# A fused chunk attention and top-1 mixture of experts: the gathered rows are turned by a DRAM scratch and VectorE instead of TensorE

## The chip, the cores and the metric

The kernel runs on one core of a Trainium2 chip. The metric is the device time of one execution in microseconds; lower is better. The profile comes from one execution that the hardware profiler recorded.

## The reference

Attention works on 4 batches, 8 heads, 768 positions of 64 numbers. Chunks of 32 queries see 8 memory keys and up to 56 keys around the chunk. Its output is laid out as 3072 tokens of 512 numbers and goes into a mixture of 8 experts, of which each token takes one:

```python
logits = x @ w_gate + modality_bias[modality_id]
e_idx = np.argmax(logits, axis=1)
...
for e in range(E):
    mask = e_idx == e
    if not mask.any():
        continue
    h = np.maximum(x[mask] @ w1[e], 0.0)          # 512 -> 1024
    out[mask] = gate_w[mask, None] * (h @ w2[e])  # 1024 -> 512
```

All of it is float32. The outputs follow the inputs' draw: how many tokens an expert gets is known only on the chip.

## The kernel before

**Stages.** The first third of the time is attention and routing: TensorE, VectorE (DVE), ScalarE (ACT) and GpSimd (POOL) go through 32 half-units of heads, and the normalized outputs go to a DRAM tensor `xd`, one row of 512 numbers and a gate for each token. Behind that come the experts, in *rows of a plan*: one row is up to 256 tokens of one expert, and a *slot* is the stretch of the program in which TensorE computes one row while the other engines prepare the next. Row 0 and row 1 are prepared while attention and routing end and in the opening slot. `slot(2)` computes row 1 and prepares row 2, `slot(3)` computes row 2, and so on: rows 2, 3, `ROW_R1`, `ROW_X`, up to seven more (`nextra`, in nested `If` blocks), and two more at the end. Two small groups of 32 tokens (`rest`) ride along in two of the slots. Short slots (`short_slot`) are skipped for this input.

**A slot.** TensorE first runs `mm1(f)` for f = 0 to 7: 12 matmuls each, 128x128 weights against 256 tokens. Float32 accuracy comes from splitting each number into a high and a low float32r part (`wh`/`wl` for weights, `xth`/`xtl` for tokens, `hh`/`hl` for the hidden layer) and adding three products. Then `mm2(f)` for f = 0 to 7: 6 matmuls each against 512 columns. ACT and DVE split the weights (`conv`): those of `w2` during `mm1`, those of the next row's `w1` during `mm2` (`prepare`).

**Tokens.** POOL gathers the next row's 2 x 128 tokens from `xd` into `xg` (`gather`). They stand with a token on each partition, and `mm1` wants a feature on each. `trans`, called from `prepare` behind `mm2(2)` and `mm2(3)`, has TensorE turn 4 blocks of 128x128 into PSUM, from where ACT and DVE write `xth` and `xtl`. `trans_rest` does the same for 32 tokens.

**Order.** TensorE, SyncE (SP) and POOL follow the order of the code, and from the opening slot on ACT and DVE too. Weights come on SP's queue, eight DMAs of 256 KB for `w1` (`load_w(row, 0)`) and eight for `w2`. Each waits until its `raw` buffer has been converted. Each is conditional: where the plan has the same expert as the row before, the register `c` is 0 and no bytes move. In `begin`, POOL stores the finished row (`store`), waits for that store, copies indices and gates (`keep`) and gathers.

Of the kernel before, what the change touches and what calls it, by code (L numbers as in the profile page):

```python
# [53 lines left out]
def tile_chunk_attention_top1_moe(  # L54
# [676 lines left out]

    def trans(half):
# [5 lines left out]
        sl = slice(2 * half, 2 * half + 2)  # L738
        nc.scalar.copy(xth[:, sl, 0:256], t)  # L739
        nc.vector.tensor_sub(xtl[:, sl, 0:256], t, xth[:, sl, 0:256].bitcast(F32))  # L740

    def trans_rest(i):
        t = bank()[:, 0:4 * NR].rearrange("p (c n) -> p c n", c=4)
        for c in range(4):
            nc.tensor.transpose(t[:, c], xgr[i][:, c * P:(c + 1) * P], ident[0:NR, 0:NR])
        nc.scalar.copy(xth[:, :, 256:], t)
        nc.vector.tensor_sub(xtl[:, :, 256:], t, xth[:, :, 256:].bitcast(F32))
# [353 lines left out]
```

## Time and profile before

| | us |
|---|---|
| median of 3 runs | 457.82 |
| lowest and highest | 456.39, 460.05 |
| the profiled execution, its own time | 456.86 |
| its span, first to last instruction | 455.1 |

The span is what the profile's rows count from; 1.8 us of the execution lie around it. The profile names TensorE's matmuls PE, its weight loads PEld. PEclk is the granted TensorE clock as a share of 2.4 GHz.

### The profile page before, as it was taken

The numbers are of one execution on the slowest core, as the hardware profiler recorded it, in microseconds if no ns is written. First come the engines' busy times: TensorE is split into PE (matmuls) and PEld (weight loads), VectorE is DVE, ScalarE is ACT, GpSimd is POOL, SyncE is SP. The second block draws the span as 40 slices with busy tenths as digits, with TensorE's granted clock in tenths as the row PEclk, the third lists the DMA queues.
The fourth block names the chain that finished last, engine by engine and source line by source line (L and its number), as shares of the span: only waits on it lengthen the run. The fifth ranks groups of instructions, "written<-read, shape, count | busy, mean of one in ns | idle before, by whom it ended". The sixth has DMA issues, their size and how long they took to land. (4 is left out here: it accounts for less than half of the span.)

```text
span 455.1 us, 11712 instructions
## 1 busy us (share of the span) xinstructions
PE 426.9 (94%) x4009; PEld 360.7 (79%) x4009; DVE 309.9 (68%) x747; ACT 261.7 (58%) x524; POOL 194.6 (43%) x374
## 2 busy tenths in 40 slices
PE   7989997999975997999999999999999999999993
PEld 4667776777754886989796987989898988898982
DVE  7989796798884799848465455766667574848430
ACT  5758674685734663747366455656565665656421
POOL 8967679769784643314052221304040404040201
PEclk9999998999996899999999999999999999999998
DMA  7899999999859402177186824202662201111101
GB/s 198 155 218 239 210 238 191 242 192 195 183 137 247 171 1 88 54 209 238 39 234 231 237 73 161 94 0 95 172 210 83 89 5 53 44 50 46 46 2 46
DMA packets 74818, 61.66 MB, mean 135 GB/s; under 512 B 36091, under 2 KB 64979, under 8 KB 74740
## 3 DMA queue, kind: packets, MB, share of 16 engines
q1 hardware_dynamic: 68000, 41.50, 39.0%
q0 software_dynamic: 5888, 19.11, 14.0%
q8 instruction: 36, 0.59, 0.6%
q14 instruction: 42, 0.34, 0.3%
q10 hardware_dynamic: 852, 0.11, 0.2%
HBM read 77.43 MB, written 12.76 MB: 198 GB/s over the span
## 5 line engine op out<-in xcount | busy, mean ns | idle before, releaser
L756 PEld LDWEIGHTS tr<-xt,w 128*128 128x128 f32 x1152 | 143.0, 191 | 6.0 <-issue 2.2
L756 PE MATMUL tr<-xt,w 128*128 128x256 f32 (+1 forms) x1152 | 144.8, 287 | 2.9 <-PEq L1062 0.8
L766 PE MATMUL av<-wh,h 128*128 128x512 f32 x384 | 128.4, 400 | 0.0
L791 POOL DMA_INDIRECT out_dram<-o,ix_now x24 | 24.3, 1014 | 159.0 <-ACT o L787 157.7
L760 DVE SCALAR_TENSOR_TENSOR h<-tr,h 128x256 fp32r<-128x256 f32 x96 | 40.5, 423 | 73.0 <-ACT h L757 54.4
L766 PEld LDWEIGHTS av<-wh,h 128*128 128x128 f32 x384 | 72.3, 188 | 17.3 <-issue 1.7
L766 PE MATMUL av<-wl,h 128*128 128x512 f32 x192 | 75.8, 395 | 0.0
L289 POOL COPY vw<-vw 24x384 f32<-24x384 f32 (+1 forms) x128 | 61.7, 521 | 20.9 <-DMA vw<-in_v_dram 19.8
L704 DVE TENSOR_TENSOR w<-raw,w 128x512 fp32r<-128x512 f32 x94 | 60.3, 683 | 14.0 <-ACT w L702 13.9
L704 DVE TENSOR_TENSOR wl<-raw,wh 128x512 fp32r<-128x512 f32 x91 | 63.4, 698 | 7.5 <-ACT wh L702 0.2
L757 ACT ACTIVATE h<-tr 128x256 fp32r<-128x256 f32 x96 | 36.8, 385 | 53.0 <-PE tr L756 32.9
L702 ACT CAST wh<-raw 128x512 fp32r<-128x512 f32 x96 | 58.8, 615 | 0.0
L702 ACT CAST w<-raw 128x512 fp32r<-128x512 f32 x96 | 54.2, 624 | 5.0 <-DMA raw<-in_moe_w_dram 3.8
L787 ACT ACTIVATE o<-av,gate_now 128x512 f32<-128x512 f32 x24 | 16.2, 690 | 47.0 <-PE av L766 37.8
L766 PEld LDWEIGHTS av<-wl,h 128*128 128x128 f32 x192 | 36.2, 189 | 7.0
L331 ACT COPY kbd<-tr 64x672 f32<-64x672 f32 x47 | 36.6, 779 | 7.0 <-PE tr L325 4.0
L339 PE MATMUL sc<-kbd,qT 128*32 128x128 f32 x768 | 27.7, 277 | 5.4 <-POOL kbd L313 4.1
L359 ACT ACTIVATE PT<-tr 128x384 f32<-128x384 f32 x32 | 15.7, 492 | 28.4 <-PE tr L357 27.9
L719 POOL DMA_INDIRECT xg<-xd,gx x24 | 26.3, 1097 | 10.0 <-POOL gx L717 6.3
L369 PE MATMUL av<-vw,PT 128*32 128x130 f32 x768 | 29.3, 283 | 1.2 <-ACT PT L359 0.6
L339 PEld LDWEIGHTS sc<-kbd,qT 128*32 128x32 f32 x768 | 19.3, 109 | 10.9 <-POOL kbd L313 6.3
L739 ACT CAST xt<-tr 128x512 fp32r<-128x512 f32 x24 | 13.9, 586 | 22.0 <-PE tr L737 12.5
(238 smaller groups left out, 525.3 us busy)
## 6 DMA issues: line engine op xcount, KB each, us to landing
raw<-in_moe_w_dram SPq DMA_DIRECT2D x192, 256.0 KB
k<-in_k_dram SPq DMA_DIRECT2D x16, 384.0 KB
q<-in_q_dram SPq DMA_DIRECT2D x16, 384.0 KB
xd<-xb POOLq DMA_DIRECT2D x16, 384.0 KB, 6.4
vw<-in_v_dram SPq DMA_DIRECT2D x32, 184.0 KB
vw<-in_mem_v_dram SPq DMA_DIRECT2D x32, 48.0 KB
vw<-in_v_dram SPq DMA_DIRECT2D x32, 6.0 KB
vw<-in_v_dram SPq DMA_DIRECT2D x32, 2.0 KB
```

Of the source, the lines that this page charges most:

```text
L289: nc.gpsimd.tensor_copy(vw[r0:r0 + 24, c + 1:c + 1 + w, h, 0:D], vw[r0 + 32:r0 + 56, c:c + w, h, 0:D])
L331: copy(dst.rearrange("p c (i j) -> p c i j", j=2)[:, :, :, j], win)
L339: nc.tensor.matmul(sc[32 * j:32 * j + 32, t * P:(t + 1) * P], qT[:, 32 * c:32 * c + 32], kbd[:, c].rearrange("p h m -> p (h m)"), start=Tr ...
L369: nc.tensor.matmul(avb[32 * j:32 * j + 32, t * W:(t + 1) * W], PT[:, t * P + 32 * j:t * P + 32 * j + 32], vw[:, c].rearrange("p h d -> p ( ...
L702: nc.scalar.copy(wh[i], raw[i])
L704: (eng or nc.vector).tensor_sub(wl[i][:, s], raw[i][:, s], wh[i][:, s].bitcast(F32))
L719: nc.gpsimd.indirect_dma_start(out=xg[t], out_offset=None, in_=xd[0:rows], in_offset=bass.IndirectOffsetOnAxis(ap=gx[:, t:t + 1], axis=0))
L756: nc.tensor.matmul(pw, wt[f][:, c * P:(c + 1) * P], x[:, c, 0:w], start=(n == 0), stop=(n == 11))
L757: nc.scalar.activation(hh[:, f], ph, AF.Relu)
L760: nc.vector.scalar_tensor_tensor(hl[:, f], ph, 0.0, hh[:, f].bitcast(F32), op0=ALU.max, op1=ALU.subtract)
L766: nc.tensor.matmul(pos[t], x, w[8 + f], start=(f == 0 and n == 0), stop=(f == 7 and n == 2))
L791: nc.gpsimd.indirect_dma_start(out=out, out_offset=bass.IndirectOffsetOnAxis(ap=ix_now[:, t:t + 1], axis=0), in_=outs[t], in_offset=None, ...
```

## The change

Rows 0 and 1 stay as they were. From row 2 on (`NWHOLE`), `send` writes the gathered tokens to a DRAM scratch `xs`, and `fetch` reads them back in four DMAs, one for each quarter of the 512 features: partition 32a + s gets quarter a of tokens s, 32 + s, 64 + s and so on. `turn` (VectorE's transpose of 32x32 blocks) makes features of the partitions, and `turned` splits the result into `xth` and `xtl`. The features then stand in another order on the partitions, so `w1` is loaded to match: four DMAs for each half of the columns, each into 32 partitions with runs of 2 KB (before: 128 partitions, runs of 512 bytes). `conv` works on blocks of that layout, and `mm1` picks its blocks accordingly. Row 2 is the first in the new layout, so its `w1` is loaded without the condition. `send` and `fetch` stand on SP's queue, behind the loads of `w1` and between the two halves of those of `w2`. POOL copies and gathers ahead of the store now, with a second pair of index and gate tiles (`ix_out`, `gate_out`) for what is stored.

```diff
@@ load_w
-        kw = {} if row == 0 else {"cond": ev[row, "c"]}
-        for f in range(8):
-            if half == 0:
+        kw = {} if row == 0 or row == NWHOLE and half == 0 else {"cond": ev[row, "c"]}
+        for f in which:
+            if half == 0 and row < NWHOLE:
...
+            elif half == 0:
+                src = w1[ds(e, 1), :, (f // 4) * DM:(f // 4 + 1) * DM]
+                c = f % 4
+                nc.sync.dma_start(
+                    raw1[32 * c:32 * c + 32, f - c:f - c + 4],
+                    src[:, c * P:(c + 1) * P].rearrange("o (c s) f -> s (o c) f", s=32), **kw)
...
+    def split(x, sl, cols):
+        nc.scalar.copy(xth[:, sl, cols], x)
+        nc.vector.tensor_sub(xtl[:, sl, cols], x, xth[:, sl, cols].bitcast(F32))
+
+    def send(rest=None):
+        if rest is not None:
+            nc.sync.dma_start(xsr[rest], xgr[rest][:, 0:DM])
+        for t in range(2):
+            nc.sync.dma_start(xs[t * P:(t + 1) * P], xg[t][:, 0:DM])
+
+    def fetch(rest=None):
+        for a in range(4):
+            sl = slice(32 * a, 32 * a + 32)
+            if rest is not None:
+                nc.sync.dma_start(xqr[sl], xsr[rest][:, a * P:(a + 1) * P])
+            nc.sync.dma_start(xq[sl], xs[:, a * P:(a + 1) * P].rearrange("(j s) d -> s j d", s=32))
+
+    def turn(half):
+        nc.vector.transpose(
+            xv.rearrange("p c (t j s) -> p t j c s", t=2, j=4)[:, half],
+            xq[:, 4 * half:4 * half + 4].rearrange("p j (c s) -> p j c s", c=4))
+
+    def turned(half):
+        sl = slice(2 * half, 2 * half + 2)
+        split(xv[:, sl], sl, slice(0, 256))
...
-    def mm1(f, rest=False):
+    def mm1(f, rest=False, first=False):
...
-            nc.tensor.matmul(pw, wt[f][:, c * P:(c + 1) * P], x[:, c, 0:w], start=(n == 0), stop=(n == 11))
+            i, j = (f, c) if first else (f - f % 4 + c, f % 4)
+            nc.tensor.matmul(pw, wt[i][:, j * P:(j + 1) * P], x[:, c, 0:w], start=(n == 0), stop=(n == 11))
@@ begin
-        if not opening:
-            for t in range(2):
-                finish(t)
-            store()
-        keep()
-        if row is not None:
-            gather(row)
+        keep(opening)
+        if row is not None:
+            gather(row)
+        if not opening:
+            for t in range(2):
+                finish(t, gate_out)
+            store(ix_out)
@@ prepare
+        if f in (2, 3):
+            turn(f - 2)
         for i in ((0, 1), (2, 3), (4,), (5,), (6, 7))[f] if f < 5 else ():
             conv(i)
-        if f in (2, 3):
-            trans(f - 2)
+        if f in (3, 4):
+            turned(f - 3)
@@ slot
-                mm1(f, rest is not None)
+                mm1(f, rest is not None, row == NWHOLE)
                 conv(8 + f)
+                if row is not None and f == 0:
+                    send(rest_next)
+                if row is not None and f == 3:
+                    if rest is None:
+                        load_w(row, 1, range(4))
+                    fetch(rest_next)
```

On SP, at the place where row 2 is loaded, this stood before: the last two loads of `w1` (line 695) and the first of `w2` (line 699); `ISA` rows set the condition and address of the load behind them.

```order
L695 ISA
L695 DMA raw_2712<-in_moe_w_dram 128x4x128
L695 ISA
L695 DMA raw_2713<-in_moe_w_dram 128x4x128
L699 ISA
L699 DMA raw_2931<-in_moe_w_dram 128x512
```

Now the same place reads as below; line 752 is `send`, line 759 `fetch`, line 704 the new load of `w1`, line 708 that of `w2`.

```order
L704 DMA raw<-in_moe_w_dram 32x4x512
L752 DMA xs<-xg_2703 128x512
L752 DMA xs<-xg_2704 128x512
L708 ISA
...
L708 ISA
L708 DMA raw_2938<-in_moe_w_dram 128x512
L759 DMA xq<-xs 32x8x128 x4
L708 ISA
L708 DMA raw_2941<-in_moe_w_dram 128x512
```

Two DMAs to DRAM have come in ahead of the loads of `w2`, and four back from it between their halves.

On DVE, in the preparing half of a slot, this stood before (line 704 is `conv`, line 740 the low part of the tokens):

```order
L704 TENSOR_TENSOR w_2703<-raw_2709,w_2702 128x512
L704 TENSOR_TENSOR w_2703<-raw_2710,w_2702 128x512
L740 TENSOR_TENSOR xt_2701<-tr,xt_2700 128x2x256
L704 TENSOR_TENSOR w_2703<-raw_2711,w_2702 128x512
L740 TENSOR_TENSOR xt_2701<-tr,xt_2700 128x2x256
```

and now (line 713 is `conv`, 762 `turn`, 746 the low part of the tokens):

```order
L713 TENSOR_TENSOR w_2708<-raw,w_2707 128x512 x4
L762 STREAM_TRANSPOSE xv<-xq 128x4x4x32
L713 TENSOR_TENSOR w_2708<-raw,w_2707 128x512
L762 STREAM_TRANSPOSE xv<-xq 128x4x4x32
L713 TENSOR_TENSOR w_2708<-raw,w_2707 128x512
L746 TENSOR_TENSOR xt_2706<-xv,xt_2705 128x2x256
L713 TENSOR_TENSOR w_2708<-raw,w_2707 128x512 x2
L746 TENSOR_TENSOR xt_2706<-xv,xt_2705 128x2x256
```

Two transposes have come into DVE's row, and the second token split stands at its end, behind the last `conv`.

## Rows read from the trace of the kernel before

**Rows 1.** The page, busy time of the engines

```profile
PE 426.9 (94%) x4009; PEld 360.7 (79%) x4009; DVE 309.9 (68%) x747; ACT 261.7 (58%) x524; POOL 194.6 (43%) x374
```

**Rows 2.** The chain that ended last, one slot: start us, us, what

```profile
401.54 11.36 PE tr L756 x96
412.89 4.20 PE av L766 x18
417.10 0.44 PE tr L737 x4
417.53 1.40 PE av L766 x6
...
419.37 5.61 PE av L766 x24
```

**Rows 3.** Timeline of PE, starts of two slots and a slot's 32 more tokens

```profile
201.98 11.37 PE L756 MATMUL tr<-xt,w 128*128 128x256 f32 x96
...
219.20 0.60 PE L737 MATMUL tr<-ident,xg 128*128 128x128 f32 x4
...
220.09 0.50 PE L766 MATMUL av<-wh,h 128*128 128x512 f32 x1
...
306.84 11.52 PE L756 MATMUL tr<-xt,w 128*128 128x256 f32 x96
```

**Rows 4.** Timeline of DVE, a slot that starts at 306.84

```profile
313.70 0.69 DVE L704 TENSOR_TENSOR wl<-raw,wh 128x512 fp32r<-128x512 f32 x1
...
319.99 3.09 DVE L704 TENSOR_TENSOR w<-raw,w 128x512 fp32r<-128x512 f32 x5
...
326.15 1.28 DVE L704 TENSOR_TENSOR w<-raw,w 128x512 fp32r<-128x512 f32 x2
```

**Rows 5.** Groups by line, engine and shape: count, busy us, mean ns

```profile
L704 DVE TENSOR_TENSOR w<-raw,w 128x512 fp32r<-128x512 f32 x94 | 60.3, 683 | 14.0 <-ACT w L702 13.9
...
L294 DVE COPY qr<-q 128x768 f32<-128x768 f32 x16 | 9.9, 617 | 1.8 <-DMA q<-in_q_dram 1.8
```

**Rows 6.** Timeline of DVE: the last instruction of the plan

```profile
181.53 0.16 DVE L521 CAST regs<-rows 64x4 int32<-64x4 f32 x1
```

**Rows 7.** Timeline of SP's queue, issues of the loads of w1

```profile
182.91 3.01 SPq L695 DMA_DIRECT2D raw<-in_moe_w_dram  x8
...
226.20 6.44 SPq L695 DMA_DIRECT2D raw<-in_moe_w_dram  x8
```

**Rows 8.** Windows of 4 us: length, busy time of engines, PEclk, DMA share, GB/s

```profile
184.00:188.00 4.00, 4.00 (x36) 4.00 (x35) 3.22 (x6) 2.51 (x6) 2.96 (x6) 1.00 0.09 18
188.00:192.00 4.00, 4.00 (x27) 3.63 (x26) 3.24 (x7) 2.93 (x8) 0.36 (x1) 1.00 0.36 115
...
244.00:248.00 4.00, 4.00 (x18) 2.43 (x17) 2.50 (x4) 2.81 (x6) 0.00 (x0) 1.00 0.92 302
```

**Rows 9.** Issues by line: us from issue to landing

```profile
xg<-xd,gx POOLq DMA_INDIRECT x24, 3.5
```

**Rows 10.** Windows of 2 us in the attention, where loads go to 32 partitions

```profile
16.00:18.00 2.00, 2.00 (x40) 1.90 (x35) 1.97 (x5) 1.29 (x3) 1.96 (x2) 1.00 0.96 102
```

**Rows 11.** Windows of 2 us, where the granted clock falls and rises

```profile
140.00:142.00 2.00, 0.88 (x5) 0.68 (x4) 0.00 (x0) 0.00 (x0) 0.51 (x2) 0.55 1.08 314
...
146.00:148.00 2.00, 2.00 (x11) 2.00 (x11) 2.00 (x6) 1.53 (x3) 0.00 (x0) 0.50 0.81 287
...
150.00:152.00 2.00, 2.00 (x21) 1.24 (x20) 0.81 (x2) 1.22 (x4) 0.86 (x1) 0.89 1.01 374
```

**Rows 12.** Windows of 1 us behind the last matmul

```profile
447.00:448.00 1.00, 0.53 (x3) 0.09 (x1) 0.00 (x0) 0.29 (x1) 0.73 (x1) 1.00 0.00 0
...
449.00:450.00 1.00, 0.00 (x0) 0.00 (x0) 0.00 (x0) 0.00 (x0) 0.64 (x1) 1.00 0.48 193
...
451.00:452.00 1.00, 0.00 (x0) 0.00 (x0) 0.00 (x0) 0.00 (x0) 0.00 (x0) 0.50 0.00 0
```

**Rows 13.** Timeline of DVE, preparing in the slot with 32 tokens more

```profile
244.33 2.50 DVE L704 TENSOR_TENSOR w<-raw,w 128x512 fp32r<-128x512 f32 x4 [2.80 <-ACT w L702]
```

More of the change, by code (lines that the diff above doesn't have):

```diff
@@ L34 @@
 HEAD = 3
+NWHOLE = 2
 LAST = 3
@@ L85, in tile_chunk_attention_top1_moe @@
     xd = dram.tile([N, XW], F32, name="xd")
+    xs = dram.tile([2 * P, DM], F32, name="xs")
+    xsr = [dram.tile([NR, DM], F32, name=f"xsr{i}") for i in range(2)]
     qf = q.rearrange("b h s d -> (b h s) d")
@@ L674, in tile_chunk_attention_top1_moe, with load_w @@
     raw, wh, wl = [None] * 16, [None] * 16, [None] * 16
-    xp = hp = w1h = w1l = xg = xth = xtl = ix = gx = hh = hl = None
-    ix_now = const.tile([P, 2], I32, name="ix_now")
-    gate_now = const.tile([P, 2], F32, name="gate_now")
+    xp = hp = raw1 = w1h = w1l = xg = xth = xtl = ix = gx = hh = hl = None
+    ix_now, ix_out = [const.tile([P, 2], I32, name=f"ix_{i}") for i in range(2)]
+    gate_now, gate_out = [const.tile([P, 2], F32, name=f"gate_{i}") for i in range(2)]
     ev = {}
-    def load_w(row, half):
+    def load_w(row, half, which=range(8)):
         if half == 0:
@@ L704, in conv, with keep @@
             (eng or nc.vector).tensor_sub(wl[i][:, s], raw[i][:, s], wh[i][:, s].bitcast(F32))
-    def keep():
+    def keep(opening):
+        if not opening:
+            nc.gpsimd.tensor_copy(ix_out, ix_now)
+            nc.gpsimd.tensor_copy(gate_out, gate_now)
         nc.gpsimd.tensor_copy(ix_now, ix)
@@ L737, in trans, with turn_rest @@
                 nc.tensor.transpose(t[:, cc, tt * P:(tt + 1) * P], xg[tt][:, c * P:(c + 1) * P], ident)
[L738 to L747, printed above, removed]
-    def mm1(f, rest=False):
+        split(t, slice(2 * half, 2 * half + 2), slice(0, 256))
+    def turn_rest():
+        nc.vector.transpose(xvr, xqr.rearrange("p (c s) -> p c s", c=4))
+        split(xvr, slice(0, 4), slice(256, 256 + NR))
+    def mm1(f, rest=False, first=False):
         w = 256 + (NR if rest else 0)
@@ L802, in tail_mm1 @@
         for c in range(4):
-            wsl = [w[:, 4 * half:4 * half + 4, c * P:(c + 1) * P] for w in (w1h, w1l)]
+            wsl = [w[:, 4 * half + c] for w in (w1h, w1l)]
             for x, w in ((xth, wsl[0]), (xtl, wsl[0]), (xth, wsl[1])):
@@ L894, in tile_chunk_attention_top1_moe @@
         if i == n:
-            mm1(0)
+            mm1(0, first=True)
         if i > n:
-            mm1(1)
+            mm1(1, first=True)
         if i >= 2 and not first:
@@ L955, in tile_chunk_attention_top1_moe @@
     conv(5)
-    mm1(2)
+    mm1(2, first=True)
     pump(99, True)
@@ L960, in tile_chunk_attention_top1_moe @@
     for f in range(3, 6):
-        mm1(f)
+        mm1(f, first=True)
     for f in range(8, 16):
@@ L964, in tile_chunk_attention_top1_moe @@
     pump(99, True)
-    mm1(6)
-    mm1(7)
+    mm1(6, first=True)
+    mm1(7, first=True)
     pos = [ps.tile([P, 512], F32, name="av", tag="av", bufs=2) for _ in range(2)]
@@ L994, in slot @@
             for f in range(8):
-                mm1(f, rest is not None)
+                mm1(f, rest is not None, row == NWHOLE)
                 conv(8 + f)
-        if rest is None and row is not None:
+                if row is not None and f == 0:
[4 more added lines that the diff above has]
+                    fetch(rest_next)
+        if opening:
             load_w(row, 1)
+        elif rest is None and row is not None:
+            load_w(row, 1, range(4, 8))
         for f in range(6):
@@ L1035, in short_slot @@
             conv(f)
+        send()
         hr = [tail_mm1(0)]
@@ L1038, in short_slot @@
             conv(f)
-        load_w(row, 1)
+        load_w(row, 1, range(4))
+        fetch()
+        load_w(row, 1, range(4, 8))
         hr.append(tail_mm1(1))
```

23 lines of the change are left out of this document (14 added, 9 removed).

## The prediction

> **What bounds the kernel now.** I began with the page's busy times: TensorE is busy for 94% of the span, the next engine, DVE, for 68% [rows 1]. The chain of waits, followed back from the end, shows a slot of the experts as an unbroken run of TensorE work: 96 matmuls of `mm1` in 11.36 us (0.118 each), then 48 of `mm2` in 4.20 + 1.40 + 5.61 = 11.21 us, and two groups of four transposes, 0.44 us each [rows 2]. That is 23.45 us, and nothing else is on the path; the timeline agrees with it, so the slot that starts at 306.84 ends at 330.29. So in this stage an instruction taken from TensorE is worth its full time, as long as the next row's weights and tokens are ready at the slot's end.
>
> **What it removes.** The transposes of 10 slots (rows 2, 3, `ROW_R1`, `ROW_X`, four more, and two at the end): 10 x 2 x 0.44 = 8.8 us. In two of them 32 more tokens are turned: from the second group of transposes to the next `mm2` it takes 220.09 - 219.20 = 0.89 us [rows 3] against 0.44, so 0.45 each and 0.9 together. All of it lies on the path: **-9.7 us**. `mm1` and `mm2` keep their counts and shapes.
>
> **What DVE and ACT get.** In a common slot DVE starts on `conv` at 319.99 and is done at 326.15 + 1.28 = 327.43 [rows 4], with short waits for ACT between. Back to back its pitch is 3.09 / 5 = 0.62 us. Ten such pieces and two transposes of T end at 319.99 + 6.2 + 0.07 + 2T. They have to be done by the slot's new end, 330.29 - 0.88, plus 8 x 0.118 = 0.95, because `xtl` is first read by the ninth matmul: 330.36. So T may be 2.05 us before any slot waits. No row shows a transpose on DVE. A plain copy costs 0.41 us for 512 columns (617 ns for 768), a difference of 512 columns 0.68 [rows 5]; if it had to pass twice it were 1.37. I take 0.68, the row with the same size, and nothing on the path. The Trainium skill ("VectorE: DVE Perf Modes", The three transpose paths) gives 311 ns for a 128x128 bf16 transpose on DVE and says that it turns only blocks of 32x32; scaled to 512 columns that is an estimate of 1.24 us, under the limit too, and no run here shows it.
>
> **What the queue gets.** A row now sends 0.52 MB to DRAM and reads it back. In a slot that loads no weights nothing is ahead of these. In one that does, the fourth load of `w2` waits for the conversion that ends at 313.70 + 0.69 = 314.39 [rows 4], and `fetch` follows. 0.26 + 0.52 MB at the weights' rate of 302 GB/s [rows 8] take 2.6 us, and what is fixed of a DMA is 3.5 us to landing [rows 9] less the 0.87 us of its 0.26 MB, or 2.6: landing at about 319.6, with DVE at `turn` at 319.99 + 4 x 0.62 = 322.5. In the slot behind the skipped short slots, SP's first load goes out at 226.20 [rows 7], with 2.1 MB of `w1`, 1.05 MB of gather and store, and 0.59 MB of `send` ahead of `fetch`: 3.74 / 0.302 = 12.4 us and 2.6 fixed give 241.2; eight issues of `fetch` at 0.38 [rows 7] and 3.0 for the last make it 247.2. DVE is done with the fourth `conv` at 246.83 [rows 13]. The first comes in time, the second 0.4 us late, inside DVE's own slack of 2 x (2.05 - 0.68) = 2.7 us: **0**. The gather goes ahead of the store on POOL, so that it no longer waits for the store's landing; POOL is free enough [rows 1], and the store is late for nobody but the end, which is as before: **0**.
>
> **Where it pays: row 2.** This row's `w1` is now loaded whatever the plan says. Before, no bytes moved for it: in the 8 us behind its issues the DMA engines carried 18 and 115 GB/s [rows 8], 0.53 MB in all, less than the slot's gather and store (1.05 MB) come to. SP can't issue earlier, as it waits for the plan's registers, written by DVE at 181.53 [rows 6]; the first load goes out at 182.91 [rows 7]. From there everything stands in one line: 2.10 MB of `w1` with gather and store (1.05 MB) beside it, then `send` (0.52 MB), whose end `fetch` waits for. At 302 GB/s that is 3.67 / 0.302 = 12.2 us, and with 2.6 fixed `send` ends at 197.7. Four issues of `fetch` at 3.01 / 8 = 0.38 us [rows 7] and 3.0 for the last one's 0.13 MB give 202.2. In before, this slot ends at 201.98 [rows 3], now at 201.1 without a wait. But DVE stands in front of `turn(0)`, and behind it four conversions, two differences and one more transpose, eight pieces in all: 8 x 0.62 = 5.0 us, 207.2, and TensorE's eight matmuls that don't need the last part begin 0.95 earlier: 206.2. A wait of 206.2 - 201.1 = 5.1 us.
>
> That took the rate of a 128-partition load. The new `w1` and `fetch` write 32 partitions, 2.62 MB of them here. The nearest rows are far apart: 302 GB/s for 128 partitions with 2 KB runs [rows 8], 102 GB/s with the engines 0.96 busy where the attention's loads go to 32 partitions in runs of 256 bytes [rows 10]. I take 280, close to the first, since the runs have the lengths of the weights' loads and the DMA engines work by the run. Then 2.62 / 0.280 - 2.62 / 0.302 = 0.7 us come on top: **+5.8 us**.
>
> TensorE idles for some 4.9 us of that in one piece. Behind the kernel's last matmul (447.5) the granted clock still reads 1.00 in the window at 449 and 0.50 in that at 451 [rows 12], so idle stretches of that length cost the clock: half of 2.4 GHz. In the attention's end it fell in the window at 140 and rose in that at 150, with TensorE fully busy at 0.50 in the window at 146 [rows 11]. Some 4.4 us of matmuls at half speed (146 to 150.4, by the 0.89 of the last window) lose half of it: **+2.2 us**, between 0 (idle too short) and 5 (half of the ten microseconds from fall to rise).
>
> **The sum.** 456.86 - 9.7 + 5.8 + 2.2 = **455.2 us**. The profiled execution stood 0.96 us below the median of 457.82, 0.2%, inside the runs' own spread, so I leave the sum as it is. A measurement of this kernel can tell about 1%, 4.6 us, from no change: below 453.2 is faster, above 462.4 slower.
>
> **Rivals.**
>
> *Row 2 comes in time for the clock* (0.30). The 2.6 us fixed are taken from GpSimd's gathers, and SP's loads may need less; in the steady run of several loads some of it overlaps. With 1.3 less in `send` and in `fetch` each the wait is 5.8 - 2.6 = 3.2 us, TensorE's idle piece 2.3, at which the row at 449 still reads a full clock [rows 12]: 456.86 - 9.7 + 3.2 = 450.4, and up to 452 with a wait that is just too short for a fall.
>
> *Quarter loads run at two thirds* (0.18). What writes 32 partitions gets 200 GB/s, the middle of rows 8 and 10. Then the loads cost 2.62 x (5.0 - 3.31) = 4.4 us more, the wait is 9.5, and with the clock the time is 456.86 - 9.7 + 9.5 + 2.2 = 458.9; 457 to 460. For it speaks that the only 32-partition rows are slow, against it their short runs. The Trainium skill ("SBUF — State Buffer", Door 1: The DMA port swizzle) states that 32 partitions reach 8 of SBUF's 16 ports and measures 189 GB/s there against 328 for 128 partitions. By that rule this rival is what happens; no row of this trace shows such a load with long runs.
>
> *Slower: `fetch` late in the loading slots as well* (0.12). One mechanism, the same quarter loads at the 102 to 130 GB/s of rows 10, at the place of row 2: at 130 the 2.62 MB cost 20.2 us instead of 8.7, the wait grows to 16.6, and the slot at 226.20, whose spare is 2.3 us, waits some 9 more: 456.86 - 9.7 + 16.6 + 2.2 + 9 = 475. It decides from a wait of 12.1 us in row 2 on (12.1 + 2.2 - 9.7 = 4.6), that is from 167 GB/s down.
>
> **How the numbers follow.** The forecast has 0.40 and covers 453 to 457.5, a little of it below 453.2 (0.05). Faster by over 1%: 0.30 + 0.05 = 0.35. Within 1%: 0.35 + 0.18 = 0.53. Slower: 0.12. The range reaches over the first rival and the second: 449.5 to 460, which leaves out the slower one and some of the fastest.
>
> **What would show it.** In the changed profile: no transposes of tokens on TensorE past the opening slot; slots of 22.6 us in the chain; one long idle of TensorE near 201, with DVE's transpose waiting for `fetch` in it, then windows with the clock at 0.50; DVE's transposes under 1 us; no other wait of TensorE for tokens. Wrong it would be if DVE's transpose took over 2 us, if TensorE waited for DVE in every slot, or if row 2's tokens came before 198.

## The result, and the profile after

Forecast: 455.2 us. The changed kernel takes 462.62 us in the median of 14 runs (459.96 to 466.05), beside 457.1 for the kernel before in the same comparison; the ratio is 1.0118, 95% interval 1.0092 to 1.0145. So it is slower by 1.2%, outside the range.

The profiled execution took 460.86 us with a span of 459.1. Page, busy times [rows 1]:

```profile
PE 421.5 (92%) x3921; PEld 354.1 (77%) x3921; DVE 322.0 (70%) x769; ACT 261.7 (57%) x524; POOL 198.6 (43%) x396
```

TensorE has 5.4 us less to do and the kernel is longer: there must be new waits. The timeline of TensorE shows where they are (start us, us, engine, line, operation, tiles, count; in brackets the idle time ahead of it and what ended it), slot 3, the slot behind the skipped short slots (R1 from here on), and two common slots [rows 3]:

```profile
206.34 0.80 PE L790 MATMUL tr<-xt,w 128*128 128x256 f32 x2 [5.41 <-ACT xt L745]
207.90 14.07 PE L790 MATMUL tr<-xt,w 128*128 128x256 f32 x94 [0.76 <-ACT xt L745]
221.81 0.39 PE L800 MATMUL av<-wh,h 128*128 128x512 f32 x1
...
235.22 0.79 PE L790 MATMUL tr<-xt,w 128*128 128x288 f32 x4 [2.06 <-ACTq L1114]
238.00 13.67 PE L790 MATMUL tr<-xt,w 128*128 128x288 f32 x92 [1.99 <-DVEq L1114]
251.51 0.39 PE L800 MATMUL av<-wh,h 128*128 128x512 f32 x1
...
315.72 11.37 PE L790 MATMUL tr<-xt,w 128*128 128x256 f32 x96
338.12 11.38 PE L790 MATMUL tr<-xt,w 128*128 128x256 f32 x96
```

A common slot is now 338.12 - 315.72 = 22.40 us and was 23.41 to 23.44. Two places wait: ahead of slot 3, for row 2's tokens, 5.41 + 0.76 us; and at line 1114, where the short slots are skipped (the join from here on). There TensorE waits 2.06 us for ACT's queue, runs four matmuls and waits 1.99 us more for VectorE's queue; before, it waited 0.85. Behind the first wait, `mm1` takes 14.07 us for 94 matmuls instead of 11.37 for 96.

Before, `mm2` of slot 3 and of R1 started at

```profile
213.18 0.39 PE L766 MATMUL av<-wh,h 128*128 128x512 f32 x1
...
239.63 0.40 PE L766 MATMUL av<-wh,h 128*128 128x512 f32 x1
```

VectorE in front of both places, same columns:

```profile
203.68 0.71 DVE L762 STREAM_TRANSPOSE xv<-xq 128x512 f32<-128x512 f32 x1 [9.82 <-DMA xq<-xs]
...
228.11 0.71 DVE L762 STREAM_TRANSPOSE xv<-xq 128x512 f32<-128x512 f32 x1 [2.01 <-DMA xq<-xs]
...
233.78 0.68 DVE L746 TENSOR_TENSOR xt<-xv,xt 128x512 fp32r<-128x512 f32 x1
```

It waits for `fetch` in row 2 and again in slot 3. SP's queue of slot 2 and slot 3 (issue only; the landing is later) [rows 7]:

```profile
182.13 4.03 SPq L704 DMA_DIRECT2D raw<-in_moe_w_dram  x8
190.86 3.58 SPq L752 DMA_DIRECT2D xs<-xg  x2
194.79 1.39 SPq L708 DMA_DIRECT2D raw<-in_moe_w_dram  x4
197.85 1.81 SPq L759 DMA_DIRECT2D xq<-xs  x4
...
216.72 0.33 SPq L750 DMA_DIRECT2D xsr<-xgr  x1
217.14 0.88 SPq L752 DMA_DIRECT2D xs<-xg  x2
...
221.24 0.50 SPq L758 DMA_DIRECT2D xqr<-xsr  x1
...
225.14 0.32 SPq L759 DMA_DIRECT2D xq<-xs  x1
```

In slot 3, `send` goes out 216.72 - 206.34 = 10.4 us into the slot, because its first DMA takes the rest's 32 tokens (`xgr`), and these are gathered late, as GpSimd shows:

```profile
210.04 1.01 POOL L825 DMA_INDIRECT out_dram<-o,ix  x1 [0.30 <-issue]
...
211.85 1.12 POOL L741 DMA_INDIRECT xgr<-xd,gxr  x1 [0.28 <-POOL gxr L740]
```

The rest's gather stands behind the store of the slot's outputs. The windows (length, busy times, granted clock, DMA share, GB/s) of row 2's loads and of the idle piece behind them [rows 8, 11]:

```profile
184.00:186.00 2.00, 2.00 (x19) 2.00 (x18) 1.53 (x4) 1.39 (x4) 1.49 (x2) 1.00 1.07 230
...
190.00:192.00 2.00, 2.00 (x10) 1.60 (x9) 1.70 (x5) 2.00 (x5) 0.00 (x0) 1.00 1.07 204
204.00:206.40 2.40, 0.06 (x1) 0.06 (x1) 2.23 (x5) 0.73 (x2) 0.00 (x0) 0.50 1.07 241
206.00:214.00 8.00, 6.90 (x31) 6.60 (x32) 4.21 (x9) 4.79 (x10) 3.57 (x5) 0.51 0.89 215
214.00:218.00 4.00, 4.00 (x36) 4.00 (x35) 2.91 (x5) 1.99 (x5) 0.00 (x0) 1.00 0.39 112
```

From 184 to 192, while row 2's `w1` comes, the DMA engines are full (1.04 to 1.09) and move 204 to 231 GB/s. The clock reads 0.50 in the window at 204 and 0.51 from 206 to 214. Behind the join it is down again:

```profile
238.00:240.00 2.00, 2.00 (x8) 2.00 (x9) 0.00 (x0) 0.00 (x0) 1.39 (x3) 0.50 0.51 101
```

**Where the time went, slot by slot.** Lengths are differences between the first `mm1` matmuls of one slot and the next; X is the slot behind R1. I use them for all kernels below, since the attention stage, which the change doesn't touch, ends differently from one profiled execution to another (slot 2 starts between 176.8 and 185.8 us), so that spans of single executions don't compare. The ratios come from the repeated runs. The profiled executions of `e5_wide_w1` and `e13_both_orders` were slow ones, of which I read the slots and rates alone. All slots of a row come from one execution, and slots and ratios agree only to some 0.6% of the time (`e9a_pool_order`: its ten slots are 4.4 us shorter than before, 1.0% of the time; its ratio says 0.35%).

| kernel | slot 2 | slot 3 | R1 | X | these four | wait of TensorE at the join | median us, before's in the same comparison | ratio, 95% interval |
|---|---|---|---|---|---|---|---|---|
| before | 24.68 | 24.79 | 28.62 | 28.04 | 106.13 | 0.85 | | |
| after | 29.53 | 28.88 | 30.71 | 27.19 | 116.31 | 2.06 + 1.99 | 462.62, 457.1 | 1.0118 [1.0092, 1.0145] |
| e1_rest_gather_first | 28.49 | 26.54 | 30.44 | 28.59 | 114.06 | 0.52 + 1.09 | 459.63, 457.78 | 1.0048 [1.0009, 1.0087] |
| e2_first_new_row_3 | 24.55 | 29.01 | 31.81 | 27.19 | 112.56 | 6.44 + 1.11 | 459.38, 457.78 | 1.0042 [1.0011, 1.0073] |
| e3_both | 24.76 | 25.72 | 31.79 | 27.71 | 109.98 | 3.15 + 1.87 | 457.35, 457.78 | 0.9992 [0.9967, 1.0016] |
| e4_spin | 28.73 | 29.43 | 30.45 | 28.06 | 116.67 | 5.22 + 0.56 | 464.81, 457.78 | 1.0144 [1.0106, 1.0182] |
| e5_wide_w1 | 24.70 | 23.06 | 30.70 | 27.19 | 105.65 | 0.49 + 1.62 | 451.71, 457.74 | 0.9888 [0.9833, 0.9944] |
| e6_row2_conditional | 23.80 | 30.86 | 30.72 | 28.13 | 113.51 | 8.28 + 1.03 | 459.98, 457.74 | 1.0038 [0.9993, 1.0083] |
| e7_before_row2_loaded | 24.58 | 24.44 | 28.62 | 28.03 | 105.67 | 0.49 | 458.88, 457.74 | 1.0035 [0.9999, 1.0070] |
| e8_token_first | 24.72 | 28.96 | 31.19 | 28.20 | 113.07 | 6.39 + 0.99 | 461.21, 457.74 | 1.0094 [1.0057, 1.0130] |
| e9a_pool_order | 23.27 | 25.71 | 31.28 | 27.19 | 107.45 | 2.66 + 1.34 | 457.0, 457.77 | 0.9965 [0.9930, 1.0000] |
| e9b_pool_order_wide | 24.81 | 24.69 | 31.54 | 27.19 | 108.23 | 2.11 + 1.34 | 455.97, 457.77 | 0.9956 [0.9925, 0.9987] |
| e9d_pool_order_row3 | 24.76 | 24.88 | 31.73 | 27.19 | 108.56 | 2.30 + 1.67 | 456.7, 457.77 | 0.9955 [0.9923, 0.9986] |
| e10_join_load | 24.30 | 25.52 | 28.62 | 28.00 | 106.44 | 1.39 | 460.06, 457.77 | 1.0037 [1.0003, 1.0070] |
| e11_rest_on_pe | 23.79 | 24.36 | 27.82 | 27.21 | 103.18 | 0.75 | 451.96, 458.16 | 0.9874 [0.9821, 0.9927] |
| e12_fetch_early | 23.80 | 25.48 | 32.05 | 27.18 | 108.51 | 2.27 + 2.14 | 454.38, 458.16 | 0.9877 [0.9826, 0.9927] |
| e13_both_orders | 23.77 | 23.92 | 27.84 | 27.21 | 102.74 | 0.80 | 453.04, 458.16 | 0.9833 [0.9775, 0.9892] |

The other six slots took 141.38 us before and 135.84 after (22.40 to 23.13 each), and stay within 0.3 us in sum of 135.84 in every kernel that has the new transposes. All ten together: 247.51 before, 252.15 after, +4.6 us, which is the measured loss of 5.5 within what the stage ahead of them scatters.

### The profile page after: what moved, and what is told of

It is laid out like the page before. It is cut to its first block, busy times and chain, and to the rows that moved or that the text cites. A ratio compares the mean times of both kernels' runs of the same rounds, so it can differ in the third digit from the quotient of the medians.

```text
span 459.1 us, 11672 instructions
## 1 busy us (share of the span) xinstructions
PE 421.5 (92%) x3921; PEld 354.1 (77%) x3921; DVE 322.0 (70%) x769; ACT 261.7 (57%) x524; POOL 198.6 (43%) x396
## 5 line engine op out<-in xcount | busy, mean ns | idle before, releaser
L790 PE MATMUL tr<-xt,w 128*128 128x256 f32 (+1 forms) x1152 | 147.4, 289 | 11.6 <-ACT xt L745 6.2
L790 PEld LDWEIGHTS tr<-xt,w 128*128 128x128 f32 x1152 | 144.6, 193 | 15.6 <-ACT xt L745 7.3
L800 PE MATMUL av<-wh,h 128*128 128x512 f32 x384 | 124.0, 396 | 0.0
L825 POOL DMA_INDIRECT out_dram<-o,ix x24 | 24.2, 1010 | 97.0 <-ACT o L821 93.6
L711 ACT CAST w<-raw 128x512 fp32r<-128x512 f32 x96 | 53.1, 619 | 5.1 <-DMA raw<-in_moe_w_dram 5.0
L342 PE MATMUL sc<-kbd,qT 128*32 128x128 f32 x768 | 29.5, 290 | 6.0 <-POOL kbd L316 6.0
L821 ACT ACTIVATE o<-av,gate 128x512 f32<-128x512 f32 x24 | 16.1, 688 | 28.7 <-PE av L800 23.4
L342 PEld LDWEIGHTS sc<-kbd,qT 128*32 128x32 f32 x768 | 20.5, 114 | 12.0 <-POOL kbd L316 7.0
L745 ACT CAST xt<-xv 128x512 fp32r<-128x512 f32 x20 | 12.4, 619 | 25.3 <-DVE xv L762 25.3
```

Source lines behind the costliest of these rows:

```text
L342: nc.tensor.matmul(sc[32 * j:32 * j + 32, t * P:(t + 1) * P], qT[:, 32 * c:32 * c + 32], kbd[:, c].rearrange("p h m -> p (h m)"), start=Tr ...
L711: nc.scalar.copy(wh[i], raw[i])
L790: nc.tensor.matmul(pw, wt[i][:, j * P:(j + 1) * P], x[:, c, 0:w], start=(n == 0), stop=(n == 11))
L800: nc.tensor.matmul(pos[t], x, w[8 + f], start=(f == 0 and n == 0), stop=(f == 7 and n == 2))
L825: nc.gpsimd.indirect_dma_start(out=out, out_offset=bass.IndirectOffsetOnAxis(ap=to[:, t:t + 1], axis=0), in_=outs[t], in_offset=None, boun ...
```

## The experiments

My theory after the result (A in the expectations): the change does what it is for in every slot without loads, and loses that in two places, row 2's forced load, and the join, where the rest's late gather holds up `send` and so VectorE. The rivals: loads into 32 partitions are slow everywhere (B); VectorE has too much to do with two transposes more (C); or row 2 alone is the cause, through the clock that falls in its wait. The theory that came out at the end has three places in one chain: row 2's load, the slow loads into 32 partitions, and the rest's trip through the scratch.

**Undoing one part.** `e1_rest_gather_first` puts the rest's gather ahead of the store:

```diff
             gather(row)
+        if rest_next is not None:
+            gather_rest(rest_next)
         if not opening:
```

> The gather of the 32 more tokens goes ahead of the store on POOL. Theory A (two places of loss: row 2's forced load with the round trip behind it, and the join behind slot 3, where the late rest gather holds up send and so DVE): the first send of slot 3 leaves about 5 us earlier, DVE no longer waits 2.0 us for fetch, and TensorE's two waits at the join (2.06 and 1.99 us) and the clock's fall there shrink; the wait before slot 3 stays at 5.4 + 0.8. Time 3 to 4.5 us below the changed kernel's, so about 458 to 459.5. Theory B (what writes 32 partitions is slow everywhere): fetch stays late behind the loads, under 1 us gained. Theory C (DVE simply has too much to do with two transposes more): no change at the join.

`e2_first_new_row_3` leaves row 2 as it was before, with TensorE's transposes and a conditional load, and uses the new way from row 3 on:

```diff
-NWHOLE = 2
+NWHOLE = 3
...
-        if f in (2, 3):
+        if f in (2, 3) and row >= NWHOLE:
             turn(f - 2)
...
+        if f in (2, 3) and row < NWHOLE:
+            trans(f - 2)
```

> Row 3 instead of row 2 is the first in the new layout, row 2 is prepared as in the kernel before; row 3 has a new expert, so its unconditional load moves no byte more. Theory A: the 5.4 + 0.8 us wait and the half clock behind it (2.9 us) vanish, 0.9 us of transposes come back: 453 to 456, a ratio to the kernel before of about 0.99 to 1.0. Theory B: row 3's w1 and fetch are quarter loads as well, so a wait of about the same size appears before row 3's computation, and the time stays above 459. Theory C: no change, since DVE has the same work in all slots but one.

`e3_both` has both edits.

> Both edits. Theory A: slots of 22.6 us from slot 3 on, no wait of TensorE for tokens: 9 x 0.88 + 0.9 = 8.8 us less than the kernel before, 448 to 450, ratio 0.98 to 0.985. Theory B: above 455. Theory C: above 455, with a wait at the join.

Measured: of the loss of 1.2%, 0.7 and 0.8 points go by one edit each and 1.3 by both, which is then as fast as before. But neither saving stays where it is made. With row 2 mended, slot 2 is 24.55 and the join waits 7.55 us. With the rest's gather first, VectorE no longer waits for `fetch` in slot 3, and TensorE's two waits at the join shrink from 4.05 to 1.61 us; the wait is then in R1, for the tokens of X. VectorE in R1 and TensorE at the start of X, in `e1_rest_gather_first`:

```profile
261.71 0.71 DVE L762 STREAM_TRANSPOSE xv<-xq 128x512 f32<-128x512 f32 x1 [5.10 <-DMA xq<-xs]
```

```profile
265.66 0.53 PE L790 MATMUL tr<-xt,w 128*128 128x288 f32 x2 [1.66 <-ACT xt L745]
```

`e3_both` on TensorE's timeline, the join:

```profile
232.68 0.80 PE L790 MATMUL tr<-xt,w 128*128 128x288 f32 x4 [3.15 <-ACTq L1116]
235.34 4.93 PE L790 MATMUL tr<-xt,w 128*128 128x288 f32 x19 [1.87 <-DVEq L1116]
```

So row 2 alone is not the cause: with it out of the way, 5.02 us of wait and a slow slot R1 (31.79) remain. Theory A falls short as well: it had 453 to 456 us for `e2_first_new_row_3` and 448 to 450 for `e3_both`, and 459.38 and 457.35 were measured, where B had them (above 459 and above 455). C had no change at the join in `e1_rest_gather_first`; there was one.

**The clock.** `e4_spin` keeps TensorE busy in row 2's wait (`spin(k)` issues k matmuls of 512 columns on an unused tile):

```diff
         mm2(7, (1,))
+        if row == 2:
+            spin(20)
```

> 20 idle matmuls of 512 columns at the end of slot 2 fill TensorE's idle piece; nothing else changes. If the clock's fall costs what the windows suggest (94 matmuls in 14.07 us instead of 11.1), mm1 of slot 3 takes 11.4 us again and the kernel gains up to 2.9 us: 459 to 460. But slot 3 is then 2.9 us shorter and fetch for row 3 comes no earlier, so some of it may turn into a longer wait at the join: between 0 and 2.9 us gained in all. If the clock is not the cause of the slow mm1, it stays at 14 us.

Timeline of TensorE, slot 3's `mm1`:

```profile
211.53 0.50 PE L790 MATMUL tr<-xt,w 128*128 128x256 f32 x2 [0.38 <-ACT xt L745]
213.09 11.45 PE L790 MATMUL tr<-xt,w 128*128 128x256 f32 x94 [1.06 <-ACT xt L745]
224.38 0.39 PE L800 MATMUL av<-wh,h 128*128 128x512 f32 x1
```

and the window over it, with the clock at 1.00:

```profile
211.50:224.40 12.90, 11.81 (x97) 11.61 (x98) 9.96 (x18) 9.04 (x19) 3.63 (x6) 1.00 0.83 218
```

The fall of the clock costs 14.07 - 11.45 = 2.6 us in these 94 matmuls, and getting it back brings nothing: the join waits 5.78 instead of 4.05, and the kernel is no faster than the changed one (1.0144 to 1.0118). TensorE had only come earlier to a place where it waits for tokens.

**The load alone.** `e6_row2_conditional` takes back only the forced load (row 2's slot then computes with weights in the old arrangement against tokens in the new order, so its part of the output differs); `e7_before_row2_loaded` adds only that load to the kernel before:

```diff
-        kw = {} if row == 0 or row == NWHOLE and half == 0 else {"cond": ev[row, "c"]}
+        kw = {} if row == 0 else {"cond": ev[row, "c"]}
```

```diff
-        kw = {} if row == 0 else {"cond": ev[row, "c"]}
+        kw = {} if row == 0 or row == 2 and half == 0 else {"cond": ev[row, "c"]}
```

> The changed kernel, but row 2's w1 is loaded under the condition again, so no byte moves for it; row 2 then computes with weights of the other layout, so its rows of the output differ from the reference's. Theory A: send leaves as soon as the gather has landed, about 189, fetch lands at 194 to 196, before DVE reaches its transpose; the 5.4 + 0.8 us wait before slot 3 and the half clock behind it vanish: slot 2 takes 22.1 to 22.3 us instead of 27.7. The join behind slot 3 still waits. 452 to 456 in all. If the round trip to DRAM itself is too long for a slot (a rival to the reload), the wait stays above 3 us.

> The kernel before, with nothing but row 2's w1 loaded without the condition. Theory A: the load has 8 us or more until its first conversion and nothing waits behind it, so the time is that of the kernel before, ratio 0.998 to 1.004. If the load costs by itself (the DMA engines' share, the gather held up), there is a wait in slot 2 and the ratio is over 1.005.

Without the load there is no wait ahead of slot 3 at all, and slot 2 is 23.80; the join then waits 9.31 us, and the time is 459.98 where 452 to 456 were expected. In the kernel before, the same load leaves each slot within 0.4 us of what it was (the ratio's interval reaches from no change to +0.7%). By the slots, a load of 2 MB is harmless by itself; it hurts where tokens stand behind it in the queue.

**The rate.** `e5_wide_w1` is `e3_both` with `w1` of rows 3 and later loaded into all 128 partitions, in the same runs of 2 KB (the features are then in the natural order, and those of the tokens in the quarters', so the output differs):

```diff
                 nc.sync.dma_start(
-                    raw1[32 * c:32 * c + 32, f - c:f - c + 4],
-                    src[:, c * P:(c + 1) * P].rearrange("o (c s) f -> s (o c) f", s=32), **kw)
+                    raw1[:, f], src[:, c * P:(c + 1) * P].rearrange("o p f -> p (o f)"), **kw)
```

> The kernel with both edits, but w1 of the rows from 3 on is loaded into 128 partitions by runs of 2 KB (256 KB each, as many bytes and packets as the quarter loads). The features then stand in natural order and no longer match the tokens', so the output differs from the reference's; the work is the same. Theory B (a load into 32 partitions runs slower): w1's 2.1 MB, which take 10 to 11 us with some 230 GB/s on the DMA engines in slot 3 and in the slot behind the join, take 7 to 8 us with about 300; fetch lands 2 to 3 us earlier, DVE's waits of 3.3, 2.4 and 1.1 us for fetch shrink to under 1, TensorE's 3.15 and 1.87 us at the join to under 2.5 in sum: 3 to 5 us less than with both edits, 453 to 454. Theory A (only the order of the queue): no difference between the two layouts of the load, within 1 us.

Windows of `e5_wide_w1` while `w1` comes:

```profile
242.00:244.00 2.00, 2.00 (x17) 2.00 (x16) 1.18 (x3) 1.38 (x6) 0.94 (x1) 1.00 1.04 355
244.00:246.00 2.00, 2.00 (x17) 2.00 (x16) 1.36 (x3) 1.33 (x5) 0.00 (x0) 1.00 1.02 356
246.00:248.00 2.00, 2.00 (x17) 2.00 (x16) 1.49 (x4) 1.21 (x4) 0.00 (x0) 1.00 1.04 398
```

The same stretch of `e3_both`:

```profile
242.00:244.00 2.00, 2.00 (x17) 2.00 (x16) 1.37 (x3) 1.12 (x4) 0.00 (x0) 1.00 1.07 189
244.00:246.00 2.00, 2.00 (x17) 2.00 (x16) 1.12 (x2) 1.33 (x6) 0.00 (x0) 1.00 1.06 212
```

355 and 356 GB/s where it was 189 and 212, with the DMA engines as full: the number of partitions written is what differs. The four slots get 4.33 us shorter (slot 3 by 2.66, R1 by 1.09, X by 0.52), and the kernel is 1.1% faster than the kernel before. That is what B expected.

**The order of the queue.** `e8_token_first` is `e3_both` with `send` first, then half of `w1`, `fetch`, the other half, and `w2` last:

```diff
+        if row is not None and row >= NWHOLE:
+            send(rest_next)
+            load_w(row, 0, range(4))
+            fetch(rest_next)
+            load_w(row, 0, range(4, 8))
```

> Both edits, and SP's queue in another order: send, the first half of w1, fetch, the second half of w1, then w2. Theory A: the tokens no longer wait behind 2.1 MB of w1 and half of w2, so DVE's transposes never wait for fetch; what stays at the join is DVE's two transposes (1.4 us) and the split of the 32 tokens (0.6), since in the kernel before DVE was done only 3.4 us ahead of TensorE there and its way past the skipped blocks takes about that: 1 to 2.5 us left. 449 to 452, ratio 0.982 to 0.988. Theory B: fetch lands earlier, but the conversions of the second half of w1 come late in its place, as the bytes are too many for their rate: above 454.

It is slower, 1.0094, as B had it, and the join waits 7.38 us. By the list of waits, ScalarE now waits 7.2 us once for a load of `w1` where VectorE had waited for tokens. Windows of quarter loads, then of `w2`:

```profile
216.00:218.00 2.00, 2.00 (x10) 1.63 (x9) 1.83 (x4) 0.82 (x2) 0.00 (x0) 1.00 1.05 203
...
222.00:224.00 2.00, 2.00 (x10) 1.62 (x9) 0.00 (x0) 0.00 (x0) 0.00 (x0) 1.00 1.04 305
224.00:226.00 2.00, 0.97 (x5) 0.44 (x3) 1.30 (x3) 1.14 (x2) 0.00 (x0) 1.00 1.05 386
```

203 and 305 to 386 GB/s in one slot of one kernel. In this order it is the weights that come late instead of the tokens.

**The quarters made elsewhere.** If GpSimd, which has time in this stage, puts each gathered row's features in the order of the quarters before they are sent, the transposed features come out in the natural order and `w1` can be loaded wide:

```diff
+    def quarter(o, x):
+        nc.gpsimd.tensor_copy(
+            o.rearrange("p (a c s) -> p a c s", a=4, c=4),
+            x[:, 0:DM].rearrange("p (c a s) -> p a c s", c=4, a=4))
...
+        if row is not None and row >= NWHOLE:
+            for t in range(2):
+                quarter(xgp[t], xg[t])
+            if rest_next is not None:
+                quarter(xgrp, xgr[rest_next])
...
-            nc.sync.dma_start(xs[t * P:(t + 1) * P], xg[t][:, 0:DM])
+            nc.sync.dma_start(xs[t * P:(t + 1) * P], xgp[t])
```

`e9a_pool_order` does so from row 2 on with the loads of the kernel before (conditional again) and the rest's gather first; `e9d_pool_order_row3` is the same with `NWHOLE = 3`; `e9b_pool_order_wide` adds the copies to `e5_wide_w1`.

> All slots from row 2 on use the scratch and VectorE's transposes, but GpSimd writes each gathered row's features in the order of the quarters before it is sent (two copies of 128 by 512 a slot, one of 32 by 512 more for a rest), so the transposes give the natural order and w1 is loaded as in the kernel before, into 128 partitions, and row 2's load is conditional again. Theory (the loss of the change is its loads into 32 partitions plus the load that was made unconditional, exposed at the join): ten slots keep 0.85 us each, the rests about 0.5 each, the join behind slot 3 costs at most 1 to 2 us more than before's 0.85: 448 to 451 us, ratio 0.980 to 0.987. Rival (the megabyte that send and fetch add to the queue is itself what makes the loading slots late, whatever form w1 has): TensorE waits 3 us or more at the join and at the slot behind the first rest, 453 to 457, ratio 0.99 to 1.00.

> As e5_wide_w1 (scratch from row 3 on, w1 of rows 3 and later in runs of 2 KB over 128 partitions, row 3's load unconditional), with GpSimd's copies in front of the send. e5_wide_w1 measured 451.7. The copies put 2 to 4 us between the gather and the send. Theory (the fetch has time to spare once w1 comes at 350 GB/s and over): join within 1 us of e5_wide_w1's 0.49 + 1.62, 451 to 453 us. Rival (the send was just in time): the fetch is that much later, join 4 to 6 us, 454 to 457.

> As e9a_pool_order with the scratch used from row 3 on only; row 2 is transposed on TensorE as in the kernel before. Theory (row 2's fetch has 8 loads fewer ahead of it once its w1 load is conditional again, so row 2 gains like the others): 0.9 to 1.2 us slower than e9a_pool_order. Rival (row 2's gather comes late behind the plan, so its scratch trip of 13 us is exposed): faster than e9a_pool_order by 1 us or more, with a wait of TensorE ahead of slot 3 in e9a_pool_order.

All three come out 0.4% ahead of before (the interval of `e9a_pool_order` reaches 1.0000). Ahead of slot 3 nothing waits any more, and X is 27.19 (28.04 before), but the join still waits 3.5 to 4.0 us and R1 is 31.3 to 31.7. So in `e9a_pool_order` the rival did better on the join and the time, though not on X. `e9b_pool_order_wide` came out in the rival's span, too: with `send` later by GpSimd's copies, the join waits 3.45 against 2.11 in `e5_wide_w1`. `e9d` against `e9a` went with the theory in the slots (+1.11), which the times can't tell.

**The join by itself.** `e10_join_load` adds work on VectorE to the kernel before, in slot 3 and in one late common slot:

```diff
+                if f == 4 and row in (HEAD, ROW_L + 1):
+                    for _ in range(3):
+                        nc.vector.tensor_sub(idle, idle, idle)
                 prepare(f)
```

> The kernel before with three subtractions of 128 by 512 more on VectorE (0.69 us each, 2.1 in sum) in two slots, put ahead of its last two conversions: in slot 3, behind which the skipped short slots join all engines, and in the slot of the last stage's first row, which is followed by a slot without a join. Theory (VectorE has no slack at the join: its last instruction of slot 3 was 3.4 us ahead of TensorE's restart, and this is the join's own length): the wait of TensorE behind slot 3 grows from 0.85 to 2.5 to 3.1 us, the other slot stays within 0.2 us of 23.42; 459.5 us, ratio 1.004. Rival (the prediction's reckoning, 2.7 us of slack in each slot): both stay, ratio 1.000.

VectorE's last instruction ahead of the join and TensorE's restart, in `e10_join_load`:

```profile
226.88 2.13 DVE L1015 TENSOR_TENSOR idle<-idle 128x512 f32<-128x512 f32 x3
228.93 1.28 DVE L704 TENSOR_TENSOR w<-raw,w 128x512 fp32r<-128x512 f32 x2
...
232.94 2.35 PE L756 MATMUL tr<-xt,w 128*128 128x288 f32 x16 [1.39 <-DVEq L1067]
```

and in the kernel before:

```profile
221.26 1.28 DVE L704 TENSOR_TENSOR w<-raw,w 128x512 fp32r<-128x512 f32 x2
...
226.77 13.02 PE L756 MATMUL tr<-xt,w 128*128 128x288 f32 x96 [0.85 <-PEq L1062]
```

Neither theory was right. From VectorE's end to TensorE's restart it takes 232.94 - 230.21 = 2.73 us where VectorE's queue is what TensorE waits for; before, where it was not, it was 226.77 - 222.54 = 4.23. So by this run VectorE had 1.5 us to spare at the join, neither none nor 2.7; of the 2.13 added, TensorE shows 0.54. In the kernels in which TensorE waits twice, 3.16 to 3.92 us pass from VectorE's end to TensorE's fifth matmul (238.00 - 234.46 = 3.54 in the changed kernel), so there it had less to spare. The late slot stayed at 23.41. (The timed ratio, 1.0037, is more than the slots show; I don't explain that part.)

**What still made slot 3 late.** `e11_rest_on_pe` is `e9a_pool_order` with the rests on TensorE again, as before; `e12_fetch_early` is `e9a_pool_order` with `fetch` behind two loads of `w2` where it was behind four; `e13_both_orders` has both.

```diff
-            if rest is not None:
-                nc.sync.dma_start(xqr[sl], xsr[rest][:, a * P:(a + 1) * P])
             nc.sync.dma_start(xq[sl], xs[:, a * P:(a + 1) * P].rearrange("(j s) d -> s j d", s=32))
...
-                turn_rest()
+                trans_rest(rest_next)
```

```diff
                     if rest is None:
-                        load_w(row, 1, range(4))
+                        load_w(row, 1, range(2))
                     fetch(rest_next)
+                    if rest is None:
+                        load_w(row, 1, range(2, 4))
```

> As e9a_pool_order, but the rests are gathered in their natural order and transposed on TensorE as in the kernel before: slot 3's queue has 1 send and 4 fetches fewer, GpSimd one copy fewer, VectorE one transpose fewer. In e9a_pool_order the fetches of slot 3 were issued from 211.72 to 218.54 and VectorE waited 2.42 us for them. Theory A (the number of DMAs between the send and the last fetch makes slot 3 late): the wait falls below 1 us, TensorE's wait at the join falls from 2.66 + 1.34 to at most 2 in sum, and slots 3 and R1 together come to 54 to 55.5 us where e9a_pool_order had 56.99. Theory B (GpSimd's copies and the gather ahead of the send make it late): at most 0.7 us of it goes, slots 3 and R1 together 56 to 57.

> As e9a_pool_order, but the queue takes the fetches behind two of the first four loads of w2 where it took them behind all four. Theory A: the fetches land 1.3 to 2 us earlier (two loads of 256 KB at 300 to 400 GB/s), VectorE's wait falls to about 0.5 to 1, the join to at most 2.5 in sum, slots 3 and R1 together 55 to 56. Theory B: the fetches wait for the send's landing instead, and little changes, 56 to 57.

> e11_rest_on_pe and e12_fetch_early together. Theory A: no wait of VectorE for the fetch in slot 3, the join at 0.85 to 1.5 as in the kernel before, no fall of the clock behind it, slot R1 at 28.0 to 28.8, all slots together 239 to 241 us where the kernel before has 247.5 and e9a_pool_order 243.1; ratio 0.982 to 0.989. Theory B: slots 3 and R1 together stay at 56 or more, ratio 0.994 to 0.997 like e9a_pool_order.

SP's queue of `e9a_pool_order` in slot 3, which starts at 202.80, and VectorE's first transpose:

```profile
207.11 0.35 SPq L749 DMA_DIRECT2D xsr<-xgrp  x1
...
211.72 0.39 SPq L757 DMA_DIRECT2D xqr<-xsr  x1
...
218.54 0.32 SPq L758 DMA_DIRECT2D xq<-xs  x1
```

```profile
221.19 0.71 DVE L761 STREAM_TRANSPOSE xv<-xq 128x512 f32<-128x512 f32 x1 [2.42 <-DMA xq<-xs]
```

The same of `e11_rest_on_pe`, slot 3 from 203.55, and TensorE behind the join:

```profile
205.85 1.58 SPq L748 DMA_DIRECT2D xs<-xgp  x2
...
212.63 1.96 SPq L753 DMA_DIRECT2D xq<-xs  x4
```

```profile
219.45 0.70 DVE L756 STREAM_TRANSPOSE xv<-xq 128x512 f32<-128x512 f32 x1
```

```profile
227.91 2.36 PE L787 MATMUL tr<-xt,w 128*128 128x288 f32 x16 [0.75 <-PEq L1115]
```

`send` goes out 2.3 us into the slot instead of 4.3, the fetches are issued within 1.96 us instead of 7.14 (211.72 to 218.86), VectorE waits for nothing, the join is at 0.75, and R1 is 27.82 where it was 31.28. The four slots are 4.27 us shorter, without the trips of two rests (0.13 MB, with one of GpSimd's copies each). VectorE still makes all 20 transposes of the rows' tokens, so theory C is out. In its trace, moving `fetch` in the queue does nothing by itself (`e12_fetch_early`: join 4.41, R1 32.05), and theory A was wrong on this part. But by the times `e12_fetch_early` is as fast as `e11_rest_on_pe`, 0.9877 to 0.9874; its profiled execution took 458.07, above its median of 454.38, and may not stand for the others. So the slots show that the rests' trip was what still made slot 3 late, and the times neither confirm nor refute it. All three beat both kernels; `e13_both_orders` has 0.9833.

## Why the prediction was wrong

**Right.** The transposes were worth what was reckoned: the six common slots lost 5.54 us, X 0.85, slot 2 0.88 by its missing transposes, slot 3 and R1 1.39 and 1.34 in their `mm2`, 10.0 in all against 9.7. VectorE's transpose takes 705 ns (T was 0.68) and costs nothing in a common slot. Row 2's chain came out close: TensorE restarts at 206.34, forecast 206.9 with the 0.7 for the rate, and the wait is 5.41 + 0.76 = 6.2 against 5.8.

**Mis-sized: the clock.** Slot 3's `mm1` lasts from 206.34 to 221.81, 15.47 us, with 0.76 of wait in it; before it was 213.18 - 201.98 = 11.20. That is 3.5 us more, where 2.2 stood; 0 to 5 was the bound. In `e4_spin`, at the full clock, the stretch takes 224.38 - 211.53 - 1.06 = 11.79, so 2.9 of the 3.5 are the clock, and 0.6 come with the late start itself.

**The step that failed: "What the queue gets" = 0.** The prediction put nothing for `fetch` coming late in the slots that load weights. In the changed kernel it comes late in slot 3, and TensorE waits for that at the join at line 1114. The term has three faults.
- The prediction wrote that the gather goes ahead of the store on POOL. That holds for a row's own tokens. The rest's gather stayed behind the store, and the rest's `send` is the first of slot 3's, so all of `send` waited for it, 10.4 us into the slot. That slot's `fetch` was never reckoned, only that of common loading slots and of R1. Moving the gather takes VectorE's wait for `fetch` out of slot 3 and 1.21 us off slot 3, R1 and X together, as part of the wait moves on to X (`e1`; the table's four slots fall by 2.25, but 1.04 of that is in slot 2, which the edit doesn't touch). With the loads wide, taking the rests off the trip saves 4.27 more in the slots (`e11`).
- VectorE's slack of 2.7 us was a common slot's. At the join `e10_join_load` shows 1.5, as TensorE waits there for VectorE's queue, 2.73 us behind VectorE's last instruction.
- The rate. 280 GB/s was taken for loads into 32 partitions, 204 to 231 were measured in row 2, 203 in `e8_token_first` and 189 and 212 in `e3_both`. In row 2 this hardly shows, and that is luck: the windows from 182 to 198 carry 3.7 MB, the bytes reckoned up to `fetch`, in 16 us, at a mean of 231 GB/s, so the low rate was made up for by 2.6 us fixed that don't show on top. In slot 3, R1 and X the rate cost 4.3 us (`e3_both` to `e5_wide_w1`). The rival of two thirds had the rate about right, but not the time (457 to 460), as it left the loading slots at nothing, too. The Trainium skill ("SBUF — State Buffer", Door 1: The DMA port swizzle) gives 189 GB/s for 32 partitions and 328 for 128; the runs agree in kind, with 189 to 231 against 355 to 398.

The bill: the join costs 2.06 - 0.85 + 1.99 = 3.2 us, and the clock falls a second time, to 0.50 in the window at 238, so that R1's first stretch, 16.29 us from 235.22 to 251.51, is 3.43 longer than before's 12.86: 1.99 of wait and 1.4 of clock. 3.2 + 1.4 + 3.5 + 6.2 + 0.3 (slot 2, not assigned) - 10.0 = +4.6, the sum of the slots. Of the difference to the forecast's -1.7, 4.6 us are the join and the clock behind it, 1.3 the slow stretch behind row 2's wait and 0.4 that wait.

**The rivals.** The slower one had the place right (loading slots wait as well) and the mechanism in part: it asked for 167 GB/s or less and put R1's `fetch` at the centre. The measured rate was above that; with a higher rate the late `fetch` still decided, in slot 3, because of the rest's late gather; in `e1_rest_gather_first`, without that, the wait is in R1, where this rival had it (5.10 us of VectorE for `fetch`). That row 2 would come in time was wrong: its wait is as forecast.

What stays open: how much of the changed kernel's wait at the join each of the three faults has by itself, as mending one moves the wait to the next (7.55 us in `e2`, 9.31 in `e6`), and why `e12_fetch_early` is faster than its slots. The rests on TensorE with weights in quarters weren't tried.

## What to carry to other kernels

An operation that is free in the steady slot need not be free where engines wait for each other's queues: reckon its last instruction there with the wait's own length (2.73 us and more here), and list for each slot that differs (the first, the one with extra rows, the one ahead of a branch) what its first DMA waits for. When two loads share a queue, what is small and late (32 tokens) delays all behind it; here it was better to keep it off the queue and spend the half microsecond of TensorE. If a wait is mended and the time doesn't follow, read the next wait in the chain before the theory is given up.

## What the runs showed of the hardware

- Loads into 32 partitions with the DMA engines full (share 1.04 to 1.21) got 189 to 231 GB/s in the windows read here, loads into 128 partitions with the same 2 KB runs 355 to 398.
- At the skipped short slots TensorE restarted 2.73 us behind VectorE's last instruction in `e10_join_load`, where it waited for VectorE's queue. In the kernels in which it waits twice, 3.16 to 3.92 us passed to its fifth matmul.
- The granted clock fell to 0.50 in a wait of 5.41 us and was back at 1.00 in the window at 214, some 8 us after TensorE resumed. At the join, waits of 0.75 and 1.39 us (`e11_rest_on_pe`, `e10_join_load`) and of 0.52 + 1.09 us (`e1_rest_gather_first`) left it at 1.00; one of 0.49 + 1.62 us (`e5_wide_w1`) took it to 0.50.
- GpSimd's reordering copy of 128 by 512 took 0.75 us, VectorE's transpose of the same size 0.705.
